# K of one more unit by transposing DMA, with the projection of group 1 spread over more slots, in a cached attention kernel on one Trainium2 core

## The chip, the cores and the metric

The kernel runs on one core of one Trainium2 chip. The metric is the device time of one execution in microseconds (us). A profiled execution also has a span, from the first to the last instruction, which is 1.7 to 3.0 us shorter than the time; so spans are compared where a difference of 1 us matters. Runs are called slow where their time is over 1.5% above the fastest of the same kernel, else fast; verdicts use fast runs only. On one core nothing shows whether a slow run is a state of the chip or a wait of the kernel that some runs have and others don't.

## The reference

A query projection, attention over the last 2048 entries of a cache, and an output projection, all in bf16:

```python
B, Sq, D = 8, 32, 1024;  Hq, Hkv, Sk, Dh = 32, 4, 8192, 128
W = min(4096, max(256, Sk // 4))                      # 2048
q = (x @ wq).reshape(B, Sq, Hq, Dh).transpose(0, 2, 1, 3)
k = jnp.repeat(k_cache[:, :, Sk - W:, :], Hq // Hkv, axis=1)
v = jnp.repeat(v_cache[:, :, Sk - W:, :], Hq // Hkv, axis=1)
p = softmax(einsum("bhqd,bhkd->bhqk", q, k) * Dh ** -0.5)
o = einsum("bhqk,bhkd->bhqd", p, v)
return o.transpose(0, 2, 1, 3).reshape(B, Sq, Hq * Dh) @ wo
```

A pair of a batch and a KV head is a unit: 32 units, numbered KV head by KV head. Eight units share a KV head, called a group here; each group has its slice of wq.

## The kernel before

A unit has 16 tiles of 128 keys, worked on in four slots of four tiles. K must stand with Dh on the partitions before TensorE can use it, and there are three ways to get it there: TensorE transposes it (units in `PE_T`), the DMA transposes it while loading (most units), or VectorE transposes 32 by 32 blocks and GpSimd moves them to their places (units in `V_T`, the "turned" units). Everything that is not scores and values is put into slots by hand:

```python
N_WARM = (8, 0, 0)
PE_T = (0, 1, 2, 3, 4)
# unit: (loaded with unit, slots of the 4 block transposes, first and last slot of the 16 moves, moves by GpSimd)
V_T = {5: (2, (5, 6, 8, 10), 10, 17, 12),
       **{u: (u - 4, range(4 * u - 16, 4 * u - 12), 4 * u - 13, 4 * u - 4, 16) for u in (8, 11, 14, 17, 20, 23, 26, 29)}}
Q_SLOTS = {1: (17, 31), 2: (38, 54), 3: (69, 83)}     # slots over which a group's projection is spread
...
    def load_unit(self, ui):                           # K and V of one unit, then raw K of turned units, then weights
        ...
        for u, at in V_T.items():
            if at[0] == ui:
                self.load_k(u)
        for p, at in zip(self.weights, W_AT):
            if at == ui:
                p()
...
        for ui, (b, g) in enumerate(self.units):
            if ui:
                self.va_copy(ui)                       # VectorE: V into the layout with a column of ones
            for c in range(NCH):                       # one slot
                ...                                    # 4 score matmuls, the exponential on ACT
                while len(pv_queue) > 2:
                    pv_queue.pop(0)()                  # 8 value matmuls of two slots earlier; at a unit's end VectorE normalises
                ...                                    # transposes of the next unit's K, if it is in PE_T
                for p in plan[ui * NCH + c]:           # projections first, then blocks and moves
                    p()
```

VectorE and GpSimd work through their own instructions in the order of the program. Where VectorE waits for one thing, everything behind it waits too (2.76 us in e7_mended below); this is what the whole case turns on. Raw K is K as it was loaded, before it is turned; PSUM is the memory that TensorE writes its results to.

Of the kernel before, what the change touches and what calls it, by code (L numbers as in the profile page):

```python
# [11 lines left out]
BF16 = mybir.dt.bfloat16  # L12
FP32 = mybir.dt.float32
# [6 lines left out]
N_WARM = (8, 0, 0)  # L20
# [3 lines left out]
PE_T = (0, 1, 2, 3, 4)  # L24

V_T = {5: (2, (5, 6, 8, 10), 10, 17, 12),
       **{u: (u - 4, range(4 * u - 16, 4 * u - 12), 4 * u - 13, 4 * u - 4, 16) for u in (8, 11, 14, 17, 20, 23, 26, 29)}}
W_AT = (3, 3, 4, 4, 8, 8, 9, 9, 11, 12, 13, 13, 14, 15, 16, 16, 18, 19, 19, 20, 22, 22, 23, 24, 25, 26, 28, 28)

Q_SLOTS = {1: (17, 31), 2: (38, 54), 3: (69, 83)}  # L30
# [74 lines left out]
class Fast:  # L105
# [101 lines left out]
    def load_unit(self, ui):  # L207

        if ui < len(self.units):
            if ui not in V_T:  # L210
                self.load_k(ui, None if ui in PE_T else 0)
            self.load_v(ui, self.nc.sync)
            if ui not in V_T and ui not in PE_T:
                self.load_k(ui, 1)
        for u, at in V_T.items():
            if at[0] == ui:
                self.load_k(u)
        for p, at in zip(self.weights, W_AT):
            if at == ui:
                p()  # L220
# [46 lines left out]
    def q_pieces(self, g):  # L267
        nc, P, DC = self.nc, self.P, self.DC
        st = {}

        def piece(hl, i):
            if i == 0:
                st["ps"] = self.ps_m.tile([P, 512], FP32, name="q_ps", tag="m")
            for c in range(i * DC // 2, (i + 1) * DC // 2):
                nc.tensor.matmul(st["ps"][:, 0:self.NQ], lhsT=self.wq_t[g, i][:, c % (DC // 2), hl * P:(hl + 1) * P],  # L275
                                 rhs=self.xT[:, c, :], start=(c == 0), stop=(c == DC - 1))
            if i == 1:
                nc.vector.tensor_copy(out=self.q_view(g)[:, :, hl, :],  # L278
                                      in_=st["ps"][:, 0:self.NQ].rearrange("p (b s) -> p b s", b=self.B))
        return [lambda h=h, i=i: piece(h, i) for h in range(self.rep) for i in range(2)]  # L280
# [31 lines left out]
    def start(self):  # L312
        nc, P = self.nc, self.P
# [3 lines left out]
        xf = self.x.rearrange("b s d -> (b s) d")  # L317
# [3 lines left out]
        nc.scalar.dma_start(out=x_sb[:, 1, :], in_=xf[P:2 * P, :])  # L321
# [25 lines left out]
        warm_up(N_WARM[0])  # L347


        def x_turn(half, pl, tag):  # L350
            ps = pl.tile([P, H, self.NT, P], BF16, name="xT_ps", tag=tag)
            for c in range(H):
                for t in range(self.NT):
                    nc.tensor.transpose(ps[:, c, t, :], x_sb[:, t, half * H + c:self.D:self.DC], self.ident[:, :])  # L354
            for i, copy in ((0, nc.vector.tensor_copy), (1, nc.scalar.copy)):
                c0 = half * H + i * H // 2
                copy(out=self.xT[:, c0:c0 + H // 2, :], in_=ps[:, i * H // 2:(i + 1) * H // 2, :, :].rearrange("p c t s -> p c (t s)"))

        x_turn(0, self.ps_m, "m")
        x_turn(1, self.ps_s, "s_ps")  # L360
# [18 lines left out]
        for c in range(self.DC):  # L379
            for h in range(self.rep):  # L380
                q_mm(c, h, 0, P if c >= Q_CUT else self.NQ)
            if c == 0:
                warm_up(N_WARM[2])
                warm_sb = self.c1.tile([P, 8], BF16, name="warm_sb")
                nc.vector.tensor_copy(out=warm_sb[:, :], in_=warm[:, 0:8])
            if c == self.DC - 3:
                tp = self.ps_s.tile([P, KT, P], BF16, name="kf_ps", tag="s_ps")
                k_turn(0)
                k_copy(0)
# [266 lines left out]
```

## Time and profile before

| | before |
|---|---|
| time, median of three runs | 185.55 us (185.06 to 186.25) |
| span of the profiled run | 183.3 us |
| TensorE busy | 178.7 us, 98% |
| ACT, VectorE, GpSimd busy | 131.6, 114.8, 94.7 us |
| first projection matmul, slot 0, unit 8, end of TensorE | 5.84, 12.92, 52.01, 180.53 us |

A row of the timeline reads: start, duration, engine, source line, operation, what it writes and what it reads, how many; then in brackets the idle time before it and what ended it. The starts of matmuls are measured and their ends are modelled, so I measure a wait of TensorE from start to start, less what the matmul itself takes; it comes out about 0.16 us longer than the bracket. The rows that matter are shown in the prediction.

### The profile page before, as it was taken

Reading aid. Unit: us, or ns where it says so; the run is one execution under the profiler, and the core shown is the slowest. Engines: PE = TensorE matmul, PEld = TensorE weight load, DVE = VectorE, ACT = ScalarE, POOL = GpSimd, SP = SyncE. Lnnn points to the kernel's source line nnn. Section 1 sums busy time; section 2 is a strip of 40 time slices with the busy share of each in tenths; the row PEclk is TensorE's granted clock in tenths of the full one; section 3 lists DMA queues with packets and bytes.
Section 4 is the critical chain, followed back from the end, with each engine's and each line's share of the span. In section 5 each row is a group of like instructions: output and inputs, shape, how many; then the busy total and the mean of one; then the engine's idle time right before and its main releaser. Section 6 shows DMA issues by size and latency. Waiting matters only on the chain.

```text
span 183.3 us, 5041 instructions
## 1 busy us (share of the span) xinstructions
PE 178.7 (98%) x2041; PEld 153.6 (84%) x2057; DVE 114.8 (63%) x266; ACT 131.6 (72%) x133; POOL 94.7 (52%) x150
## 2 busy tenths in 40 slices
PE   7999999999999999999999999999999999999993
PEld 2899999999999999987878999987787888888843
DVE  0238899975584774685567558647755865365363
ACT  2218999777799877777786687787877888888800
POOL 2000019759839959929945980896299279600000
DMA  6999999999999999999999999989999999960003
GB/s 173 392 405 407 397 402 367 186 249 397 258 307 303 384 240 325 401 246 249 378 380 227 374 389 224 245 327 386 242 371 345 216 272 286 229 185 1 0 32 93
DMA packets 52954, 51.73 MB, mean 282 GB/s; under 512 B 39744, under 2 KB 40256, under 8 KB 52928
## 3 DMA queue, kind: packets, MB, share of 16 engines
q1 hardware_dynamic: 52352, 50.90, 98.3%
q10 hardware_dynamic: 576, 0.49, 0.8%
q8 instruction: 16, 0.26, 0.6%
q14 instruction: 10, 0.08, 0.1%
HBM read 41.42 MB, written 0.52 MB: 229 GB/s over the span
## 4 chain that ended last, share of the span: by engine, by line
PE 96%; DMA 2%; issue 1%; DVE 0%
PE o_ps L478 32%; PE s_ps L467 31%; PE op_ps L295 14%; PE q_ps L275 11%; PE q_ps L375 4%; DMA x_sb<-in_x_dram 2%; PE tp L236 2%; PE xT_ps L354 1%; PE kf_ps L368 1%; DVE o_t L305 0%; PE cnt_ps L532 0%
## 5 line engine op out<-in xcount | busy, mean ns | idle before, releaser
L469 ACT ACTIVATE pT<-s_ps 128x1024 bf16<-128x1024 f32 x128 | 128.8, 1025 | 32.4 <-PE s_ps L467 31.4
L261 POOL TENSOR_SCALAR kTv<-kb 32x512 bf16<-32x512 bf16 x140 | 93.7, 670 | 63.8 <-PE s_ps L467 37.3
L478 PE MATMUL o_ps<-va,pT 128*128 128x129 bf16 x1024 | 78.8, 220 | 0.1
L478 PEld LDWEIGHTS <-pT 128*128 128x128 bf16 x1024 | 68.5, 98 | 3.1
L467 PE MATMUL s_ps<-QT,kT 128*128 128x256 bf16 x368 | 55.2, 273 | 0.2
L467 PEld LDWEIGHTS <-kT 128*128 128x128 bf16 x368 | 34.8, 98 | 10.3
L295 PE MATMUL op_ps<-wo_sb,OT 128*128 128x512 bf16 (+2 forms) x128 | 32.7, 352 | 0.6
L275 PE MATMUL q_ps<-xT,wq_sb 128*128 128x256 bf16 x192 | 28.1, 273 | 0.0
L409 DVE COPY va<-v_sb 128x2048 bf16<-128x2048 bf16 x32 | 25.3, 789 | 0.1
L251 DVE STREAM_TRANSPOSE kb<-k_raw 128x512 bf16<-128x512 bf16 x36 | 23.8, 685 | 0.0
L415 DVE RECIPROCAL RL_all<-o_ps 128x2 f32<-128x2 f32 x32 | 5.2, 164 | 27.5 <-PE o_ps L478 27.5
L467 PE MATMUL s_ps<-QT,kTv 128*128 128x256 bf16 x144 | 21.6, 272 | 0.0
L420 DVE TENSOR_SCALAR o_sb<-o_ps,RL_all 128x128 bf16<-128x128 f32 x64 | 19.5, 346 | 1.1
L467 PEld LDWEIGHTS <-kTv 128*128 128x128 bf16 x144 | 13.9, 98 | 5.1
L278 DVE CAST QT<-q_ps 128x256 bf16<-128x256 f32 x24 | 9.8, 406 | 13.4 <-PE q_ps L275 13.4
L275 PEld LDWEIGHTS <-wq_sb 128*128 128x128 bf16 x192 | 17.0, 98 | 1.2
L422 DVE STREAM_TRANSPOSE OT<-o_sb 128x256 bf16<-128x256 bf16 x32 | 14.3, 445 | 1.1
L295 PEld LDWEIGHTS <-OT 128*128 128x128 bf16 x144 | 11.4, 98 | 2.3 <-DVE OT L422 0.2
L302 DVE TENSOR_TENSOR oacc<-op_ps,oacc 128x512 f32<-128x512 f32 x8 | 5.5, 682 | 7.4 <-PE op_ps L295 7.4
L375 PE MATMUL q_ps<-xT,wq_sb 128*128 128x256 bf16 (+1 forms) x80 | 7.7, 251 | 0.0
L375 PEld LDWEIGHTS <-wq_sb 128*128 128x128 bf16 x80 | 6.7, 98 | 0.7
L236 PE MATMUL tp<-ident,k_raw 128*128 128x128 bf16 x64 | 5.9, 219 | 0.0
(30 smaller groups left out, 36.6 us busy)
## 6 DMA issues: line engine op xcount, KB each, us to landing
v_sb<-in_v_cache_dram SPq DMA_DIRECT2D x30, 512.0 KB, 7.0
wo_sb<-in_wo_dram SPq DMA_DIRECT2D x16, 512.0 KB, 6.5
wq_sb<-in_wq_dram SPq DMA_DIRECT2D x13, 512.0 KB, 7.3
k_raw<-in_k_cache_dram SPq DMA_DIRECT2D x13, 512.0 KB, 5.9
wq_sb<-in_wq_dram SPq DMA_DIRECT2D x6, 256.0 KB, 4.6
v_sb<-in_v_cache_dram SPq DMA_DIRECT2D x4, 256.0 KB, 4.8
kT<-in_k_cache_dram SPq DMA_TRANSPOSE x36, 6.5
k_raw<-in_k_cache_dram SPq DMA_DIRECT2D x2, 256.0 KB, 5.8
```

The costliest lines, as they stand in the source:

```text
L251: nc.vector.transpose(out=st["kb"][:, sl, :], in_=self.k_raw[ui][:, sl, :])
L261: nc.gpsimd.tensor_scalar(out=out, in0=in_, scalar1=1.0, scalar2=1.0, op0=ALU.mult, op1=ALU.mult)
L275: nc.tensor.matmul(st["ps"][:, 0:self.NQ], lhsT=self.wq_t[g, i][:, c % (DC // 2), hl * P:(hl + 1) * P], rhs=self.xT[:, c, :], start=(c == ...
L278: nc.vector.tensor_copy(out=self.q_view(g)[:, :, hl, :], in_=st["ps"][:, 0:self.NQ].rearrange("p (b s) -> p b s", b=self.B))
L295: nc.tensor.matmul(ps[:, 0:w], lhsT=self.OT[:, gq, c, t * P:(t + 1) * P], rhs=self.wo_t[gq][:, c, n0:n0 + w], start=(k == 0), stop=(k == 7))
L375: nc.tensor.matmul(qs[h // 2][:, h % 2, n0:n1], lhsT=self.wq_t[0, c // H][:, c % H, h * P:(h + 1) * P], rhs=self.xT[:, c, n0:n1], start=(c ...
L409: self.nc.vector.tensor_copy(out=self.va[ui % 3][:, :, 0:self.Dh], in_=self.v_sb[ui][:, :, :])
L420: nc.vector.tensor_scalar(out=o_sb[:, qt, :, :], in0=o_ps[:, qt, 0:Dh].rearrange("p (i c) -> p c i", c=4), scalar1=rl[:, ui * QT_N + qt:ui ...
L422: nc.vector.transpose(out=self.OT[:, g * QT_N:(g + 1) * QT_N, :, b * self.Sq:(b + 1) * self.Sq], in_=o_sb[:, :, :, :])
L467: nc.tensor.matmul(s_ps[:, jj, :], lhsT=self.kT[ui][:, c * CJ + jj, :], rhs=q_u, start=True, stop=True)
L469: nc.scalar.activation(out=pT[:, :, :], in_=s_ps[:, :, :], func=ACT.Exp, bias=0.0, scale=self.scale)
L478: nc.tensor.matmul(o_ps[:, qt, 0:self.VW], lhsT=pT[:, jj, qt * P:(qt + 1) * P], rhs=va[:, j, 0:self.VW], start=(j == 0 and qt == 0), stop= ...
```

## The change

The intent: take 16 transposes from TensorE, the bound. K of unit 4 goes through the transposing DMA. That takes longer (K and V of unit 4 landed in 3.0 us instead of 2.6 in e5_k4_alone), and so, it seems, group 1's weights are loaded ahead of the raw K of the turned units, and the projection of group 1 starts three slots earlier and needs the second half of the weights later (first half for four heads, then second half). The turned units' blocks and moves move one slot back, unit 8's three. Separately, x is loaded and turned by row tiles, and a warm-up matmul goes.

```diff
-N_WARM = (8, 0, 0)
+N_WARM = 7
-PE_T = (0, 1, 2, 3, 4)
+PE_T = (0, 1, 2, 3)
 V_T = {5: (2, (5, 6, 8, 10), 10, 17, 12),
-       **{u: (u - 4, range(4 * u - 16, 4 * u - 12), 4 * u - 13, 4 * u - 4, 16) for u in (8, 11, 14, 17, 20, 23, 26, 29)}}
+       8: (4, range(19, 23), 22, 30, 16),
+       **{u: (u - 4, range(4 * u - 15, 4 * u - 11), 4 * u - 12, 4 * u - 4, 16) for u in (11, 14, 17, 20, 23, 26, 29)}}
-Q_SLOTS = {1: (17, 31), 2: (38, 54), 3: (69, 83)}
+Q_SLOTS = {1: (14, 31), 2: (38, 54), 3: (69, 83)}
 # load_unit: the loop over self.weights now stands before the loop over V_T
 # q_pieces: two heads share a PSUM bank and one cast
-                     st["ps"] = self.ps_m.tile([P, 512], FP32, name="q_ps", tag="m")
+                     st[k] = self.ps_m.tile([P, 2, self.NQ], FP32, name="q_ps", tag="m")
 ...
+        n = 4 if g == 1 else 2
+        return [... for h0 in range(0, self.rep, n) for i in range(2) for h in range(h0, h0 + n)]
 # start
-        nc.scalar.dma_start(out=x_sb[:, 1, :], in_=xf[P:2 * P, :])
+        nc.sync.dma_start(out=x_sb[:, 1, :], in_=xf[P:2 * P, :])
 ...
+        def x_turn(t):
+            ps = self.ps_s.tile([P, 2, self.DC, P], BF16, name="xT_ps", tag="s_ps")
             for i, copy in ((0, nc.vector.tensor_copy), (1, nc.scalar.copy)):
+                for c in range(H):
+                    nc.tensor.transpose(ps[:, i, c, :], x_sb[:, t, i * H + c:self.D:self.DC], self.ident[:, :])
+                copy(out=self.xT[:, i * H:(i + 1) * H, t * P:(t + 1) * P], in_=ps[:, i, 0:H, :])
```

## The prediction

> **What bounds the kernel now.** I read the page first: the busy line and the chain that ended last.
>
> ```profile
> PE 178.7 (98%) x2041; PEld 153.6 (84%) x2057; DVE 114.8 (63%) x266; ACT 131.6 (72%) x133; POOL 94.7 (52%) x150
> ...
> PE 96%; DMA 2%; issue 1%; DVE 0%
> ```
>
> TensorE is busy for 98% and is 96% of the chain, so nothing but TensorE's own work, and the 4.5 us before it can begin, makes the time. Next I read TensorE in order of time, since a share of busy time does not say whether it runs at its rate.
>
> ```profile
> 28.55 0.60 PE L467 MATMUL s_ps<-QT,kT 128*128 128x256 bf16 x4
> 28.99 0.62 PE L478 MATMUL o_ps<-va,pT 128*128 128x129 bf16 x8
> 29.44 0.39 PE L236 MATMUL tp<-ident,k_raw 128*128 128x128 bf16 x4
> 29.66 0.60 PE L467 MATMUL s_ps<-QT,kT 128*128 128x256 bf16 x4
> ```
>
> I call four score matmuls, the eight value matmuls of two chunks earlier and whatever is woven in between a slot; a unit has four slots (unit u starts at slot 4u). Start to start, scores take 0.44 us, values 0.45, four transposes 0.22: a bare slot is 0.89 us, one with four transposes 1.11, one with four projection matmuls (0.44) 1.33. I followed all 128 slots and found no wait over 0.03 us; where 0.22 us seemed lost, a first output-projection matmul is missing from the records. The change can thus win only work taken from TensorE and an earlier start, and it loses wherever a feeder's slack is used up. The slack is in the other engines' timelines. GpSimd, which assembles the turned K of units 5, 8, 11, ..., 29 (the last line from near the end of the run):
>
> ```profile
> 27.03 8.77 POOL L261 TENSOR_SCALAR kTv<-kb 32x512 bf16<-32x512 bf16 x12 [25.46 <-PE s_ps L467]
> 38.44 11.77 POOL L261 TENSOR_SCALAR kTv<-kb 32x512 bf16<-32x512 bf16 x16 [2.64 <-PE s_ps L467]
> 53.18 11.65 POOL L261 TENSOR_SCALAR kTv<-kb 32x512 bf16<-32x512 bf16 x16 [2.97 <-DVE kb L251]
> ```
>
> ```profile
> 147.41 11.74 POOL L261 TENSOR_SCALAR kTv<-kb 32x512 bf16<-32x512 bf16 x16 [4.21 <-DVE kb L251]
> ```
>
> Each assembly is 16 moves, 11.7 us, and starts when VectorE has finished the fourth block transpose of that unit. Unit 8's ends at 50.21 and TensorE reads it at 52.01 (slack 1.8 us); unit 29's ends at 159.15 and is read at 159.85 (slack 0.7):
>
> ```profile
> 52.01 0.60 PE L467 MATMUL s_ps<-QT,kTv 128*128 128x256 bf16 x4
> ```
>
> ```profile
> 159.85 0.60 PE L467 MATMUL s_ps<-QT,kTv 128*128 128x256 bf16 x4
> ```
>
> VectorE, nearly full from 20 to 40 us:
>
> ```profile
> 27.82 1.04 DVE L409 COPY va<-v_sb 128x2048 bf16<-128x2048 bf16 x1
> ...
> 35.77 0.39 DVE L278 CAST QT<-q_ps 128x256 bf16<-128x256 f32 x1
> 36.08 1.28 DVE L251 STREAM_TRANSPOSE kb<-k_raw 128x512 bf16<-128x512 bf16 x2
> 37.29 0.39 DVE L278 CAST QT<-q_ps 128x256 bf16<-128x256 f32 x1
> 37.59 0.69 DVE L251 STREAM_TRANSPOSE kb<-k_raw 128x512 bf16<-128x512 bf16 x1
> ```
>
> The V copy of unit 3 ends at 28.86 and is read by the value matmul at 28.99: slack 0.1 us. Unit 8's fourth block ends at 38.28, and GpSimd starts 0.15 later. Last, the head:
>
> ```profile
> 0.75 3.70 DMA x_sb<-in_x_dram
> 4.50 1.33 PE xT_ps L354 x16
> 5.84 5.40 PE q_ps L375 x48
> ```
>
> **What the Trainium skill says.** "TensorE: Matmul & The Clock Gate", section "Back-to-back issue gap", gives N/2.4 + 2.5 ns warm: 109 ns for 256 columns, 56 for 128. The trace agrees (0.44 us for four scores). Its Part 1 gives N/1.2 while the array is cold; the eight warm-up matmuls of 512 start 427 ns apart, and x's transposes go from 118 to 62 ns apart near 4.8 us, so the changed kernel's earlier first transposes may still be cold. "SBUF — State Buffer", section "Who interferes with whom", says that a VectorE copy in a two-port mode and a GpSimd instruction shut each other out for a whole instruction. The trace agrees: V copies take 0.65 us alone and 1.04 beside GpSimd, and a move grows from 0.61 to about 1.0. "DMA: Bandwidth & Descriptors", "Latency and other measured facts", has 261 GB/s for a DMA transpose with a non-contiguous dimension; here halves of 256 KB land 0.8 to 2.4 us after the transfer before them, where 512 KB of plain K takes 1.3.
>
> **The change part by part.** I read the waits of the changed program from its instruction order and semaphores.
>
> *x by row tiles.* Both tiles now share one queue, so tile 0 should land near 3.9 us (both land at 4.45 and 4.63 now; 256 KB take about 0.65) and tile 1 near 4.6. But each tile's PSUM buffer is now filled in two halves with VectorE's copy of the first half between, and the second four transposes wait for that copy. Per copy: 0.26 us from the start of the last transpose to the copy (5.11 to 5.37 now), 0.425 for the copy, 0.05 back. The chain: 3.95, + 0.24 to 0.36 to the fourth transpose, + 0.74, + 0.42 to the eighth transpose of the next batch, + 0.74, + 0.24 for four more: the projection starts at 6.35 to 6.5 instead of 5.84. **+0.55 us.** The removed warm-up matmul (0.43) is before x arrives and is worth nothing by itself.
>
> *K of unit 4.* 16 transposes of 56 ns leave TensorE: **-0.89 us**, 0.45 of it in slots 12 and 13, 0.45 in slots 14 and 15 (in whose place projection comes earlier, the same work). Two VectorE copies of 0.65 go too. The DMA side: two transposed halves cost 1.6 to 3 us instead of 1.3; K of unit 4 should land by 29 to 31 us and is read from 31 on, its second half two slots later, so it should not be waited for. ACT follows two short slots: its exponentials went 0.91 us apart at slots 33 to 37, which cost TensorE only 0.03 a slot.
>
> *Who pays for shorter slots 12 and 13.* VectorE's work up to the V copy of unit 3 is the same, in the same order, tied to the end of unit 0. TensorE now wants it 0.45 us earlier; slack was 0.1. **+0.37 us** of waiting in slot 14.
>
> *Group 1 over slots 14 to 29.* Same 64 matmuls. Casts are one per two heads: four of about 0.6 us by their spacing (448 columns: 0.53 now) for eight of 0.31.
>
> *Unit 8's K.* This is the large term. Its blocks move from slots 16 to 19 to slots 19 to 22, and in VectorE's order blocks three and four now stand behind unit 4's normalisation and the second cast, which wait for slot 21's value and projection matmuls. I count from the start of slot 22 (S). Value matmuls of slot 21 done at S - 0.25; VectorE, just done with block two, does the normalisation (1.22 us in the trace from reciprocal to the end of the transpose), ending at about S + 1.2; cast 0.6; blocks 0.61 + 0.69; 0.15 to GpSimd: start at S + 3.25. Sixteen moves: 11.75, and 0.05 to TensorE: S + 15.05. Without a wait TensorE reaches unit 8 after eight slots of 1.327 and two of 0.89: S + 12.4. **Wait +2.65 us** (in the kernel before GpSimd starts at S - 0.3). All sixteen moves are needed, since every score contracts over all of them.
>
> *Later turned units.* Their blocks and moves are one slot later. Units 14 to 26 have 2.4 us or more of slack against about 1.2. Unit 11 is helped by unit 8 being late. Unit 29 has 0.7: its fourth block goes behind the V copy of unit 26, from 146.52 to about 147.7, so GpSimd runs to about 160.3: **+0.5 us.**
>
> *Weights ahead of raw K; casts in pairs in groups 2 and 3.* Nothing on the path.
>
> Sum: 0.55 - 0.89 + 0.37 + 2.65 + 0.5 = **+3.2 us**, 185.55 to about 188.7. I put it at 188.6.
>
> **The rivals.** (1) *The intended gain*: TensorE stays full, the transposes go (-0.9) and x arriving by rows gives -0.3: 184.4 us. For it speaks that TensorE is the bound and that the author set unit 8's slots by hand; against it, slot 22 to unit 8 leaves 12.4 us for a GpSimd job of 11.7 that cannot start before S + 2.2 even with VectorE idle. So I hold this for very unlikely. (2) *A DMA wait in place of the one removed*: the two transposed halves sit early in a saturated stream (about 400 GB/s to 32 us), and if they took 2.4 us each, the second half of group 1's weights would land near 34.5 us, where slot 18 wants it: up to 1 us more; unit 8's last blocks stand behind that projection on VectorE, so the later wait would not swallow it: 189.6. (3) *Waits that overlap less badly*: if VectorE is through with unit 4's normalisation sooner and GpSimd meets fewer V copies, the wait for unit 8 is 1.5 us and unit 29 comes out even: 187. (4) *The clock*: a gap of over 3 us on TensorE could throttle it again; at 2.65 us I expect not; with it 190.5.
>
> **Range and chances.** The terms I am least sure of are unit 8 (1.3 to 3.2), the head (0.3 to 0.8) and unit 29 (0 to 0.9). Together they span 186.9 to 189.8 for 8 in 10. Two per cent slower begins at 189.3, under one sigma above my figure: 0.24. Faster by 2% would need 181.8, more than the removed work: 0.01. Within 2%: 0.75.
>
> **What would show it.** In the changed profile: L467 on kTv at unit 8 preceded by an idle TensorE of about 2.6 us released by GpSimd; GpSimd's second run of 16 moves starting about 3 us after slot 22; VectorE's x copies with TensorE idle some 0.7 us before two batches of transposes, and the first q_ps matmul near 6.4; a wait of some 0.4 us on the V copy of unit 3; no wait on a DMA at unit 4. I am wrong if GpSimd's second run starts by about 41 us, or if TensorE shows no idle time before unit 8.

## The result, and the profile after

The changed kernel took 191.41 us (median of four runs, 190.13 to 193.17, one of them slow; a fifth took 190.28) against 185.31 (184.82 to 186.25) for the kernel before on the same chip. The ratio is 1.029, 95% interval 1.021 to 1.037: slower. Ratios here are the mean time of one kernel's fast runs over that of the other's of the same rounds, so they are not quite the ratio of the medians. I had predicted 188.6 and a range up to 189.8.

The page of the changed kernel, busy time, the row of TensorE's load in 40 slices, the granted clock, and the chain:

```profile
PE 181.5 (95%) x2024; PEld 155.1 (81%) x2040; DVE 112.7 (59%) x252; ACT 131.9 (69%) x133; POOL 94.0 (49%) x150
...
PE   7899999999949999999999999999999999999993
...
PEclk9999999999996999999999999999999999999999
...
PE 84%; POOL 6%; DVE 5%; issue 2%; ACT 1%; ACTq 0%
```

TensorE has 17 instructions less and is busy 2.8 us longer. There is a hole in slice 12, the clock is down in the slice after it, and GpSimd and VectorE are now in the chain. In the kernel before TensorE was 96% of it and there was no row of the clock at all. The row tells nothing of the head, since the profile records the clock only from its first change on; there the spacing of the matmuls tells. The hole, in the timeline of the changed kernel (VectorE, GpSimd, TensorE):

```profile
42.75 0.65 DVE L280 CAST QT<-q_ps 128x512 bf16<-128x512 f32 x1
43.32 1.28 DVE L252 STREAM_TRANSPOSE kb<-k_raw 128x512 bf16<-128x512 bf16 x2
44.75 11.95 POOL L262 TENSOR_SCALAR kTv<-kb 32x512 bf16<-32x512 bf16 x16 [6.50 <-issue]
56.76 0.61 PE L466 MATMUL s_ps<-QT,kTv 128*128 128x256 bf16 x4 [2.61 <-POOL kTv L262]
57.66 0.94 PE L466 MATMUL s_ps<-QT,kTv 128*128 128x256 bf16 x4
58.39 1.07 PE L477 MATMUL o_ps<-va,pT 128*128 128x129 bf16 x8
```

Slot 22 starts at 41.59. GpSimd's second run starts 3.16 us after it (it started at 38.44, 0.3 before slot 22, in the kernel before), so unit 8 begins 2.77 us late by start to start. Then the same eight value matmuls that took 0.62 us take 1.07. The table of stretches says why; its eighth column is the granted clock:

```profile
core 0: us, PE busy (x) PEld busy (x) DVE busy (x) ACT busy (x) POOL busy (x), PEclk, DMA share, GB/s
...
57.77:61.18 3.41, 3.41 (x26) 2.93 (x24) 1.61 (x5) 2.51 (x3) 3.10 (x6) 0.50 1.30 143
```

For 3.41 us after the wait TensorE ran at half its clock. The head, in the same timeline:

```profile
3.72 0.63 PE L359 MATMUL xT_ps<-ident,x_sb 128*128 128x128 bf16 x4
4.39 0.42 DVE L360 COPY xT<-xT_ps 128x512 bf16<-128x512 bf16 x1 [0.26 <-PE xT_ps L359]
4.87 1.01 PE L359 MATMUL xT_ps<-ident,x_sb 128*128 128x128 bf16 x8 [0.52 <-DVE xT L360]
...
6.40 0.59 PE L359 MATMUL xT_ps<-ident,x_sb 128*128 128x128 bf16 x4 [0.51 <-DVE xT L360]
...
6.78 3.48 PE L378 MATMUL q_ps<-xT,wq_sb 128*128 128x256 bf16 x16
```

The two waits for VectorE's copy are there, and the projection starts at 6.78. But 16 of its matmuls take 3.48 us, 0.21 each, where they took 0.11: the clock is released (from half to full rate) only at 9.98, the first change on record. And the wait for the V of unit 3 in slot 14 (0.37 by start to start):

```profile
31.42 0.61 PE L477 MATMUL o_ps<-va,pT 128*128 128x129 bf16 x8 [0.21 <-DVE va L408]
```

Where the 7.3 us between the two profiled spans (183.3 and 190.6) come from, by landmarks of TensorE:

| stretch | before | after | difference | made of |
|---|---|---|---|---|
| start to slot 0 | 12.92 | 15.43 | +2.51 | 0.94 later start, 1.57 half clock |
| slot 0 to 14 | 15.63 | 15.18 | -0.45 | eight transposes gone |
| slot 14 to 22 | 10.19 | 10.98 | +0.79 | +0.37 wait, -0.45 transposes, +0.87 two projection pieces done earlier |
| slot 22 to unit 8 | 13.27 | 15.17 | +1.90 | +2.77 wait, -0.87 the same two pieces |
| unit 8 to slot 127 | 120.22 | 122.22 | +2.00 | +1.60 half clock (slots 33 to 35), +0.44 wait at unit 29 |
| slot 127 to the end | 11.07 | 11.62 | +0.55 | after TensorE's end |

Three of the other four runs of the changed kernel had spans of 188.4 to 188.7, the fourth 190.2 (this is the one called slow: its time is 2.97 us longer than its span); so the profiled one is at the long end. The head is the part that varies from run to run in the experiments; the other four were not profiled.

### The profile page after: what moved, and what is told of

Same layout as the page of the kernel before. It is cut to its first block, busy times and chain, and to the rows that moved or that the text cites. A ratio compares the mean times of both kernels' runs of the same rounds, so it can differ in the third digit from the quotient of the medians.

```text
span 190.6 us, 4997 instructions
## 1 busy us (share of the span) xinstructions
PE 181.5 (95%) x2024; PEld 155.1 (81%) x2040; DVE 112.7 (59%) x252; ACT 131.9 (69%) x133; POOL 94.0 (49%) x150
## 4 chain that ended last, share of the span: by engine, by line
PE 84%; POOL 6%; DVE 5%; issue 2%; ACT 1%; ACTq 0%
PE o_ps L477 27%; PE s_ps L466 26%; PE op_ps L298 14%; PE q_ps L277 9%; POOL kTv L262 6%; PE q_ps L378 4%; PE warm_ps L349 2%; DVE kT L239 1%; DVE kb L252 1%; PE xT_ps L359 1%; DVE va L408 1%; DVE o_sb L419 1%; PE tp L237 1%; ACT pT L468 1%; PE kf_ps L371 0%
## 5 line engine op out<-in xcount | busy, mean ns | idle before, releaser
L477 PE MATMUL o_ps<-va,pT 128*128 128x129 bf16 x1024 | 79.7, 221 | 0.3 <-DVE va L408 0.2
L477 PEld LDWEIGHTS <-pT 128*128 128x128 bf16 x1024 | 69.3, 99 | 3.7 <-issue 0.4
L466 PE MATMUL s_ps<-QT,kTv 128*128 128x256 bf16 x144 | 22.5, 281 | 2.9 <-POOL kTv L262 2.6
L466 PEld LDWEIGHTS <-kTv 128*128 128x128 bf16 x144 | 14.1, 101 | 8.6 <-POOL kTv L262 3.5
L277 PEld LDWEIGHTS <-wq_sb 128*128 128x128 bf16 x192 | 16.9, 98 | 1.1
L280 DVE CAST QT<-q_ps 128x512 bf16<-128x512 f32 x12 | 8.0, 669 | 7.8 <-PE q_ps L277 7.8
L378 PE MATMUL q_ps<-xT,wq_sb 128*128 128x256 bf16 (+1 forms) x80 | 9.2, 278 | 0.0
L378 PEld LDWEIGHTS <-wq_sb 128*128 128x128 bf16 x80 | 7.5, 108 | 1.4
L375 DVE COPY kT<-kf_ps 128x1024 bf16<-128x1024 bf16 x2 | 1.4, 692 | 8.2 <-PE kf_ps L371 8.2
```

The costliest lines, as they stand in the source:

```text
L277: nc.tensor.matmul(st[k][:, hl % 2, :], lhsT=self.wq_t[g, i][:, c % (DC // 2), hl * P:(hl + 1) * P], rhs=self.xT[:, c, :], start=(c == 0 a ...
L280: nc.vector.tensor_copy(out=self.q_view(g)[:, :, 2 * k:2 * k + 2, :].rearrange("p b h s -> p h b s"), in_=st[k][:, :, :].rearrange("p h (b ...
L378: nc.tensor.matmul(qs[h // 2][:, h % 2, n0:n1], lhsT=self.wq_t[0, c // H][:, c % H, h * P:(h + 1) * P], rhs=self.xT[:, c, n0:n1], start=(c ...
L466: nc.tensor.matmul(s_ps[:, jj, :], lhsT=self.kT[ui][:, c * CJ + jj, :], rhs=q_u, start=True, stop=True)
L477: nc.tensor.matmul(o_ps[:, qt, 0:self.VW], lhsT=pT[:, jj, qt * P:(qt + 1) * P], rhs=va[:, j, 0:self.VW], start=(j == 0 and qt == 0), stop= ...
```

## The experiments

Seventeen kernels ran; all gave correct results. Medians are of all runs, ratios of fast runs. The kernel before ran along in each set: 185.22 in the first (the first four rows), then 185.97 (four), 186.11 (two), 185.29 (two), 185.33 (three), 185.59 (two).

| run | median us | ratio (95% interval) | TensorE's waits in the profiled run, us |
|---|---|---|---|
| e1_copies_after | 189.74 | 1.024 (1.016 to 1.031) | slot 14 0.37, unit 8 2.77, unit 29 0.42 |
| e2_warm8 | 190.71 | 1.029 (1.024 to 1.034) | the same, and two of 0.72 in the head |
| e3_blocks_early | 188.44 | 1.015 (1.012 to 1.019) | slot 14 0.37, slot 22 0.60, unit 11 1.14, unit 29 0.42 |
| e4_fill | 188.76 | 1.022 (1.016 to 1.028) | slot 14 0.37, unit 29 0.20 (unit 8 filled) |
| e5_k4_alone | 187.09 | 1.005 (0.999 to 1.010) | slot 14 0.36, slot 17 2.34 |
| e6_head_alone | 186.19 | 1.003 (0.999 to 1.007) | the head only |
| e8_k4_late_moves | 186.62 | 1.002 (0.998 to 1.007) | slot 17 0.59 |
| e7_mended | 187.38 | 1.005 (1.000 to 1.009) | slot 19 1.54, slot 31 0.30, slot 58 0.45 |
| e10_k4_weights_first | 186.53 | 0.999 (0.993 to 1.005) | slot 18 0.24, slot 19 0.28 |
| e11_mended_again | 188.39 | 1.010 (1.004 to 1.016) | slot 22 0.20, slot 31 0.29, slot 58 1.95 |
| e12_k4_earlier_blocks | 186.22 | 1.002 (0.998 to 1.006) | slot 11 0.57, slot 58 2.07, slot 70 0.33 |
| e13_unit8_late_alone | 186.04 | 1.004 (1.000 to 1.008) | unit 8 0.96 |
| e14_q_and_unit8 | 190.55 | 1.026 (1.023 to 1.030) | slot 14 1.02, unit 8 2.77 |
| e15_q_alone | 186.49 | 1.005 (1.001 to 1.008) | slot 14 1.02, slot 43 0.19 |
| e16_k4_first_at_4 | 185.44 | 1.000 (0.997 to 1.004) | slot 17 0.17, slot 19 0.28, slot 39 0.80 |
| e17_k4_and_end | 185.59 | 0.999 (0.995 to 1.003) | slot 18 0.26, slot 19 0.29 |
| e18_end_alone | 186.38 | 1.004 (0.999 to 1.008) | slot 12 0.14 |

Slow runs left out of the ratios: one each of e1, e2, e5, e7 and e10, two of six of e8, three of eight of e12; none of the kernel before. The profiled runs of e5 and e12 are among them, with waits over 2 us that belong to the kernel. So these ratios show the kernels at their better, and a ratio near 1 there does not mean that every run is. The table leaves out waits in the head before slot 0, but for e2; they are told below.

### The head and the clock

**e1_copies_after**: the changed kernel, all eight transposes of a row tile before its two copies.

```diff
-            for i, copy in ((0, nc.vector.tensor_copy), (1, nc.scalar.copy)):
+            for i in range(2):
                 for c in range(H):
                     nc.tensor.transpose(ps[:, i, c, :], ...)
+            for i, copy in ((0, nc.vector.tensor_copy), (1, nc.scalar.copy)):
                 copy(...)
```

> The changed kernel with one edit: in x's turn all eight transposes of a tile are issued before the two copies, so TensorE no longer waits for VectorE in the middle of a tile. Theory (the two pauses of 0.7 us, 4.15 to 4.87 and 5.7 to 6.4 us, delay the first projection matmul and leave the clock window too idle to be released before 9.98 us): no pause over 0.4 us, first projection matmul near 5.6 us instead of 6.78, matmuls of 256 columns 109 ns apart from about 6.6 us at the latest, slot 0 at about 12.7 to 13.0 instead of 15.43, time down by 2 to 2.5 us; the wait for unit 8's K stays at 2.5 to 2.9 us. Rival (one warm-up matmul fewer is what keeps the clock low): the pauses go, but matmuls stay 213 ns apart until near 10 us, gain under 1 us.

The two pauses went, the clock was released at 5.24 us, the projection started at 6.02 and slot 0 at 13.55. That is 1.9 us better than the profiled run of the changed kernel and over 0.5 short of what I expected, for two reasons. Tile 1's copy by VectorE (5.54 to 5.96) still stands between the last transpose and the projection, 0.4 us; and a wait of 0.45 us for weights came at 9.51 us, which I had not thought of. The rest of the change, unit 8 included, was as before.

**e2_warm8**: the changed kernel with the eighth warm-up matmul back (`N_WARM = 8`).

> The changed kernel with eight warm-up matmuls as in the kernel before, everything else unchanged. Theory (pauses, not the number of warm-up matmuls): first transposes at 4.2 instead of 3.72 us, pauses unchanged, full clock again only near 10 us; same time or up to 0.5 us longer. Rival (the eighth warm-up matmul releases the clock): 109 ns spacing from the start of the projection, slot 0 near 13.5, 1.5 to 2 us faster. The free-running clock window can make single runs differ by over 1 us, so the profile decides before the times do.

No gain in time: 1.029. But the clock was released at 6.24 here and not near 10, with the same two pauses. My expectation missed that the release moves from run to run by itself. It was at 9.98 in the changed kernel, and at 3.74, 5.18 and 3.81 in e3, e4 and e6, which have the same head; in ten looks at kernels with the old head it lay between 3.75 and 6.66. Slot 0 started at 15.43, 13.57, 13.47 and 13.88 with the new head (mean 14.1), at 13.51 to 13.72 in the three looks with the order of e1, and at 12.77 to 13.46 in eleven with the old head (mean 13.1).

**e6_head_alone**: the kernel before with only the new head (the diff of the change in `start`, and `N_WARM = 7`).

> The kernel before with only the head of the changed kernel (x on one queue, by row tiles, a copy between the two batches of transposes, seven warm-ups). My theory (the two pauses cost 0.6 to 0.9 us, and where the free-running window of the clock falls badly over them, up to 1.6 us of half clock more): first projection matmul at 6.1 to 6.8 instead of 5.84, slot 0 between 13.5 and 15.4 instead of 12.92, times spread over more than 1 us and the median 0.7 to 2 us above before (186 to 187). Rival (the head's loss is made up later, because other engines' feeds get slack): the same time as before, 185.2. A second rival (all runs of it are bad by the full 2.5 us): 187.7 with little spread.

Spans of 183.8 to 185.8 with a median of 184.15, against 183.4 for the kernel before on that chip: +0.75, at the low edge of what I expected; the ratio of 1.003 is hardly outside the noise. So the head costs 0.5 to 1 us, and the 2.51 of the profiled run were a bad fall of the clock. The second rival (always the full 2.5) is out. What it costs with a quick clock is not the pauses alone. In e6 the projection starts only 0.27 us later than before, and then it waits for weights:

```profile
10.29 1.92 PE L375 MATMUL q_ps<-xT,wq_sb 128*128 128x256 bf16 x16 [0.52 <-DMA wq_sb<-in_wq_dram]
```

That is 0.68 us by start to start, and slot 0 is 0.96 late. The piece landed at 10.24; in the kernel before it landed at 8.65 and was wanted at about 9.3. SyncE issues it at 3.55 instead of 3.08, as both tiles of x now stand in front of it; the rest of its delay I can't place. The same wait (0.38 to 0.63 us) is in e1, e3, e7 and e11, and in no look with the old head; where the projection starts at 6.4 or later (e2, e4, the changed kernel) it is not seen. So a quicker start, as in e1, gains little by itself.

**e4_fill**: the changed kernel with dummy matmuls in front of unit 8's first scores, which depend on nothing.

```diff
+                if ui == 8 and c == 0:
+                    fill = self.ps_m.tile([P, 512], FP32, name="fill_ps", tag="m")
+                    for _ in range(12):
+                        nc.tensor.matmul(fill[:, :], ...)     # operands are constant ones
+                    fill_sb = self.c1.tile([P, 8], BF16, name="fill_sb")
+                    nc.vector.tensor_copy(out=fill_sb[:, :], in_=fill[:, 0:8])
```

> The changed kernel with twelve dummy matmuls of 512 columns (2.6 us at full clock) put just before unit 8's first scores, where TensorE waits 2.77 us for GpSimd. Theory (the idle wait itself, not the work after it, halves the clock from 57.77 to 61.18 us): unit 8 starts at the same time (56.6 to 56.9 if the head is as slow as in the profile), but the half-clock window after it is gone: about 1.6 us faster, all of it in slots 33 to 35. Rival (slots 33 to 35 are slow for another reason, such as GpSimd and VectorE sharing a port): those slots stay at 1.6, 1.7 and 1.0 us.

TensorE in e4, around unit 8:

```profile
52.24 2.57 PE L467 MATMUL fill_ps<-const-bfloat16-1.0 128*128 128x512 bf16 x11
54.80 0.61 PE L472 MATMUL s_ps<-QT,kTv 128*128 128x256 bf16 x4
55.24 0.62 PE L483 MATMUL o_ps<-va,pT 128*128 128x129 bf16 x8
```

Unit 8 starts no earlier (41.33 us after slot 0 in both), but behind it TensorE runs at full rate, in all four runs (mean clock 0.998 or more). The median is 2.65 us below the changed kernel's; the profile puts 1.6 of it on the clock and the rest on the head, which fell well here. Useless work in the gap is better than none, so the half clock follows from the idle time and not from anything that unit 8 does. (Twelve matmuls were put in; the profile holds eleven, as some records can be missing.)

How much idle time it takes can be read from the traces. In every trace in which the clock is on record, the stretches between two changes of it are multiples of 3.413 us (51.20 in e14 is 15 of them, 129.71 in the changed kernel is 38). I conclude that the clock is decided window by window; the grid of windows can then be laid from the first release. What lies of a wait in one window:

| kernel | wait | window | idle in it | half clock after it |
|---|---|---|---|---|
| changed | 53.99 to 56.76 | 54.36 to 57.77 | 2.40 | yes |
| e5 | 32.93 to 35.27 | 33.02 to 36.43 | 2.25 | yes |
| e14 | 53.54 to 56.30 | 54.27 to 57.68 | 2.04 | yes |
| e11 | 84.63 to 86.59 | 83.16 to 86.57 | 1.94 | no |
| e1 | 52.11 to 54.87 | 53.02 to 56.44 | 1.85 | no |
| e12 | 84.71 to 86.78 | 85.11 to 88.52 | 1.67 | no |
| e2 | 52.71 to 55.48 | 54.03 to 57.44 | 1.45 | no |

About 2.0 us of idle time in one window halves the next; a wait of 2.77 us does so when the windows fall right. If the windows fall freely, that is the share of positions in which one window holds over 2.0 us of the wait: ((3.413 - 2.77) + 2 x (2.77 - 2.0)) / 3.413 = 64%, an estimate from the numbers of this table. Counted by a mean clock of 0.991 or less it was 13 of 17 runs: five of five of the changed kernel, two of four of e1 and of e2, four of four of e14. Nine of nine against four of eight leaves open whether the windows do fall freely. This table was made after the runs; no run was made to test the limit itself.

The same grid tells when the clock is released in the head. In all 18 traces with a record of it, the release comes at the end of the first window that holds little idle time: 0.86 us at most (e2, one pause and the beginning of the other). Windows before it held 0.95 us or more, the time before the first matmul included. In the changed kernel the window from 3.16 to 6.57 holds both pauses, 1.44 us, and the release is one window late; in e4, with the same pauses, the window from 1.77 to 5.18 holds one of them, 0.72, and the clock is released. This too was read afterwards and not tested by an edit.

### Unit 8, and what the slots really cost

**e3_blocks_early**: the changed kernel with unit 8's blocks and moves where they were.

```diff
-       8: (4, range(19, 23), 22, 30, 16),
+       8: (4, range(16, 20), 19, 28, 16),
```

> The changed kernel with unit 8's block transposes and moves back in slots 16 to 19 and 19 to 28. Theory (blocks three and four stood behind slot 21's cast on VectorE): fourth block done near 40.4 instead of 44.6 us, GpSimd's sixteen moves from 40.6 to 52.3, no wait before unit 8 (TensorE reaches it near 54.0), and no half clock at 57.8 to 61.2; 2.8 + 1.6 = 4.4 us faster in the profile. Rival (unit 8's raw K comes too late, being loaded behind the weights): VectorE stands waiting for that load before block one, and a wait before unit 8 of over 1 us stays.

The wait before unit 8 went, and so did the half clock. But two waits took its place:

```profile
PE s_ps L466 <- POOL kTv L262: 1.0, 1, 1.0
PE o_ps L477 <- DVE va L408: 0.6, 2, 0.4
```

(The columns of this view are the us waited in sum, how often, and the longest; e3 here.) Unit 11 now waits 1.14 us for GpSimd, whose blocks the change had moved back one slot and which the wait of unit 8 had covered; and slot 22 waits for the V of unit 5, since VectorE stood idle 2.05 us until 35.87 for unit 8's raw K. That raw K arrives late because the weights now come first. So of the 4.4 us that unit 8 and the clock had cost in the profile, some 2.5 (1.029 less 1.015, of 185 us) came back.

**e13_unit8_late_alone**: the kernel before with that one line of the change, unit 8 at slots 19 to 22.

> The kernel before with unit 8's blocks at slots 19 to 22 and its moves from slot 22, and nothing else. My theory: the fourth block stands behind unit 4's normalisation and a cast of 0.4 us, GpSimd's second run starts 2.9 to 3.2 us after the start of slot 22, and unit 8 waits 2.4 to 2.8 us. The clock is halved for 3.413 us after it (1.6 us more) in those runs in which a window of 3.413 us of the clock holds over 2.0 us of the wait, which for a free phase is 40 to 60% of the runs: 187.6 to 190 against before's 185.2 to 186. Rival (the wait comes from the wide casts and the late raw K of the whole change, not from the slots): a wait of under 1.5 us.

The rival was right on the size. GpSimd and TensorE in e13:

```profile
41.34 11.44 POOL L262 TENSOR_SCALAR kTv<-kb 32x512 bf16<-32x512 bf16 x16 [5.66 <-PE s_ps L468]
...
52.84 0.61 PE L468 MATMUL s_ps<-QT,kTv 128*128 128x256 bf16 x4 [0.79 <-POOL kTv L262]
```

A wait of 0.96 us, no half clock, +0.4%. So the slots of the blocks alone are a third of the term.

**e14_q_and_unit8** and **e15_q_alone**: the kernel before with the projection of group 1 as the change has it (banks of two heads, slots 14 to 30), with and without unit 8 at slots 19 to 22.

> The kernel before with two parts of the change: group 1 projected over slots 14 to 30 in banks of two heads, and unit 8's blocks at slots 19 to 22. My theory: the wait of 0.96 us that the blocks' slots alone gave grows by the two projection pieces that TensorE has behind it already at slot 22 (0.87), by the wider cast before the fourth block (0.3 to 0.45), and by 0 to 0.45 for one more V copy beside GpSimd's moves: 2.1 to 2.8 us, and in about half of the runs half a clock for 3.413 us after it. Time 187.3 to 189.5 against before's 185.3 to 186. Rival (what made the wait longer in the whole change is the late raw K of unit 8 and the late V of unit 5): the wait is 0.9 to 1.3 us, ratio 1.005.

> The kernel before with group 1 projected over slots 14 to 30 in banks of two heads, unit 8's blocks left at slots 16 to 19. My theory: the projection alone costs nothing, as it is the same 64 matmuls and unit 8's K is started early: no wait over 0.3 us before unit 8 (GpSimd starts at 38.4 to 39, is done by 50.7, and TensorE is there at 51.1 at the earliest or 52.0, depending on where the pieces lie), ratio 0.998 to 1.003. Rival (wide casts and banks of two heads make TensorE wait for PSUM or for the second half of the weights, which lands at 32.2): a new wait of 0.4 us or more between slots 14 and 22, ratio over 1.003.

TensorE in e14:

```profile
56.30 0.61 PE L470 MATMUL s_ps<-QT,kTv 128*128 128x256 bf16 x4 [2.60 <-POOL kTv L262]
...
57.64 1.02 PE L481 MATMUL o_ps<-va,pT 128*128 128x129 bf16 x8
```

The wait is 2.77 us and the half clock behind it is there in all four runs, exactly as in the changed kernel. These two parts together reach 1.026; each alone makes only 1.004 and 1.005. That this is near the whole change's 1.029 is partly luck, since e14 has a wait of 1.02 us in slot 14 (below) where the changed kernel has one of 0.37 for another reason; the proof is the same wait before unit 8, to 0.01 us, and the same half clock. The reckoning from 0.96 to 2.77: TensorE takes 12.39 us from slot 22 to the end of slot 31 instead of 13.27, because two pieces of projection are behind it already (0.88); GpSimd starts 3.16 us after slot 22 instead of 2.72, behind a normalisation of unit 4 that begins 0.21 us later and a cast that takes 0.65 instead of 0.39 (0.44); and its 16 moves end 0.5 us later relative to their start, since they fall on three V copies instead of two. That is the sum of my theory; the split is read from the two traces, and no run has the wide casts without the early pieces. In e15 the rival was right as well, with a wait that my theory had not, 1.02 us in slot 14:

```profile
PE q_ps L276 <- DVE kT L238: 0.9, 1, 0.9
```

The projection in slot 14 wants a PSUM buffer of the pool that unit 4's transposes are still using, and waits for VectorE's copy of K. In the changed kernel unit 4 has no such transposes and there is no such wait. So it seems that the early projection needs K of unit 4 to be out of the way.

### K of unit 4 by DMA

**e5_k4_alone**: the kernel before with `PE_T = (0, 1, 2, 3)`.

> The kernel before with only the K of unit 4 loaded through the transposing DMA. My theory: this part alone is worth the 0.89 us of transposes less about 0.37 us that slot 14 then waits for VectorE's copy of the V of unit 3, so about 184.7 against 185.2 (ratio 0.997), with that one wait in the trace, no DMA wait at unit 4, and no half clock anywhere (no wait near 2 us). Rival (the transposed halves disturb the saturated load stream): a DMA wait appears between slots 16 and 32 and the time is 185.2 or more.

The wait in slot 14 was 0.36 as expected, but the rival came with it. TensorE in e5, at slots 17 and 18:

```profile
35.27 0.39 PE L275 MATMUL q_ps<-xT,wq_sb 128*128 128x256 bf16 x2 [2.18 <-DMA wq_sb<-in_wq_dram]
...
36.38 1.01 PE L275 MATMUL q_ps<-xT,wq_sb 128*128 128x256 bf16 x4
```

The last piece of group 1's weights landed at 35.22, wanted at 32.93, and the half clock followed. In the kernel before the same piece landed at 32.17 and was wanted at about 33.2. The stream of loads is full until about 38 us: K and V of unit 4 together took 3.0 us there instead of 2.6, and two pieces of weights each took about 1.1 us longer than usual in this run (2.29 and 2.57 us after the landing ahead of them instead of 1.3 to 1.4), which I cannot account for; single loads of 512 KB that take 2.6 to 2.7 us stand in other traces too (one landing at 17.82 in the kernel before, one at 35.49 in e8). The next kernel shows another look.

**e8_k4_late_moves**: e5 with VectorE's four moves of unit 5 put behind the copy of the V of unit 3 (`5: (2, (5, 6, 8, 10), 13, 18, 12)`).

> As the kernel with K of unit 4 alone, and with the moves of unit 5 spread over slots 13 to 18, so that VectorE's four of them come behind its copy of the V of unit 3. My theory: the slot-14 wait goes from about 0.37 to under 0.1, and the whole 0.89 us is kept: 184.3 to 184.5 (ratio 0.995). Rival (the moves of unit 5 then end too late, and slot 20 waits): 184.7 or more, with a wait on kTv at unit 5. This would be the version that beats both.

Slot 14 no longer waited. The weights landed at 32.78 and were waited for by 0.59 us in the profiled run; in two of six runs the mean clock was 0.989 and 0.991 (189.8 and 190.0 us, both called slow and not in the ratio), so the wait was probably longer there. No gain: 1.002.

**e10_k4_weights_first**: K of unit 4 by DMA, the loop over the weights ahead of the raw K as in the change, unit 5's moves at slots 12 to 15, unit 8's blocks at `(18, 18, 19, 19)`.

> The kernel before with K of unit 4 by transposing DMA, group 1's weights loaded ahead of the raw K of unit 8 (as the change has it), the moves of unit 5 at slots 12 to 15 and the blocks of unit 8 at slots 18 and 19, ahead of anything that waits for unit 4's last values. The two looks at K of unit 4 without this order waited 2.34 and 0.59 us at slot 17 for the last piece of the weights (landed 35.22 and 32.78, wanted at about 31.9). My theory: with the order turned round it lands one K transfer (1.3 to 2.5 us) earlier, so the wait is 0 to 1 us, no half clock in most runs, unit 8 does not wait (its raw K lands near 34 to 35, GpSimd starts near 38.5, 50.3 at the end against 51.2 wanted), slot 22 may wait up to 0.5 us for the V of unit 5: 184.8 to 186 against before's 185.2 to 186, ratio 0.995 to 1.003. Rival (the K of unit 4 costs the saturated load stream more than its transposes cost TensorE, whatever the order): waits on DMA of 0.9 us or more, ratio 1.003 or more.

The weights came in time (32.00). What was left were 0.24 us for the V copy of unit 4 and 0.28 for unit 5's last move by GpSimd: VectorE had no idle time from 23 to 38 us. Ratio 0.999.

**e12_k4_earlier_blocks**: e10 with unit 5's blocks at `(5, 6, 7, 8)` and moves at 12 to 16.

> As the kernel with K of unit 4 by DMA and the weights first, but the blocks of unit 5 one and two slots earlier (slots 5, 6, 7, 8) and VectorE's four moves of it at slots 12, 14, 15 and 16, so that only three stand before the copy of the V of unit 4 and GpSimd starts sooner. In the run before this one TensorE waited 0.24 us at slot 18 for that copy and 0.28 at the end of slot 19 for GpSimd's last move of unit 5 (27.49 to 36.17). My theory: both waits go to under 0.1, and the profile shows 0.6 to 0.9 us less from slot 0 to the end of TensorE's work than before's 167.6 (180.53 - 12.92): 166.7 to 167.0; time 0.3 to 0.5% under before (the noise from run to run is 1 us, so the verdict will be same). Rival (VectorE, without idle from 23 to 38 us, is the bound there, and the blocks moved forward only push other copies back): a new wait of 0.3 us or more at slots 9 to 14 and 167.3 or more.

The rival was right: those two waits went and one of 0.57 us at slot 11 came, for a copy of K. There was also a wait of 2.07 us at slot 58, in the profiled run, that has nothing to do with unit 5. VectorE in e12:

```profile
82.16 0.71 DVE L252 STREAM_TRANSPOSE kb<-k_raw 128x512 bf16<-128x512 bf16 x1 [4.60 <-DMA k_raw<-in_k_cache_dram]
...
84.28 1.88 DVE L252 STREAM_TRANSPOSE kb<-k_raw 128x512 bf16<-128x512 bf16 x3
86.08 0.65 DVE L410 COPY va<-v_sb 128x2048 bf16<-128x2048 bf16 x1
```

The first block of unit 17 waits 4.6 us for its raw K, which stands behind weights in the queue (it landed at 82.06; in e10, with the same order, at 79.41, and no wait), and the V copy that TensorE needs stands behind it. Three of the eight runs were slow at full clock and are not in the ratio of 1.002.

**e16_k4_first_at_4**: e10 with the order turned round only in unit 4's loads.

> As the kernel with K of unit 4 by DMA and the weights first, with the order turned round for unit 4's loads only. In the last run with the order turned round everywhere, TensorE waited 2.07 us at slot 58, where VectorE's copy of V of unit 14 stood behind a block of unit 17 whose raw K came late behind weights. My theory: no wait at slot 58 in any run, 0.2 to 0.6 us at slots 18 and 19 as before, so TensorE's work from slot 0 to its end is 167.2 to 167.5 (before 167.6), no run over 1% above its fastest but for the launch, ratio 0.996 to 1.002. Rival (K of unit 4 by DMA is a loss by its own disturbance of the loads): waits over 0.9 us in sum and ratio over 1.003.

No wait at slot 58; 0.45 at slots 17 to 19, and a new one of 0.80 for K of unit 10 in slot 39, which the other runs seem not to have (five spans of six at 183.2 to 183.8). Ratio 1.000.

### Mending the changed kernel

**e7_mended**: the changed kernel with the order of e1, unit 8 at slots 16 to 19, the other turned units back by one slot, unit 5's moves at slots 13 to 17.

> The changed kernel with four mends: all transposes of an x tile before its copies, unit 8's blocks and moves back at slots 16 and 19, the other turned units' back by one slot, the moves of unit 5 at slots 13 to 18. My theory: the waits before units 8, 11 and 29 and at slot 14 go (each under 0.1), the wait at slot 22 of about 0.6 us (VectorE: V copy of unit 5 behind a block and a wide cast) stays, the head stays 0.6 behind, K of unit 4 gives 0.9: 185.2 to 186.2 (ratio 1.00 to 1.005), no half clock. Rival (a wait is left that I don't know of, as the wide casts make VectorE late elsewhere): over 187.

187.38: the waits before units 11 and 29 and at slot 14 went and that before unit 8 was down to 0.30, but there was one of 1.54 us at slot 19. VectorE in e7:

```profile
36.06 0.71 DVE L252 STREAM_TRANSPOSE kb<-k_raw 128x512 bf16<-128x512 bf16 x1 [2.76 <-DMA k_raw<-in_k_cache_dram]
...
37.96 0.29 DVE L260 COPY kTv<-kb 32x512 bf16<-32x512 bf16 x1
```

Unit 8's first block waits 2.76 us for raw K, and the last moves of unit 5, which TensorE needs at slot 20, stand behind it.

**e11_mended_again**: e7 with unit 5's moves at slots 12 to 15 and unit 8's blocks at `(18, 18, 19, 19)`.

> The changed kernel with all transposes of an x tile before its copies, the moves of unit 5 at slots 12 to 15, the blocks of unit 8 at slots 18 and 19, and the other turned units' blocks and moves back by one slot. In the mended kernel before this one unit 5 was read 1.54 us late, since VectorE's last moves for it stood behind a block of unit 8 that waited for its raw K (loaded behind the weights, landing near 34.7). My theory: that wait goes, as the four moves of VectorE are now in front; what stays is the head (0.6), up to 0.6 us at slot 22 for the V of unit 5 and 0.45 at slot 58: 185.3 to 186.5, ratio 1.00 to 1.005, no half clock. Rival (blocks at slots 18 and 19 wait for raw K as well and hold the casts of the projection): a wait of over 1 us between slots 18 and 22, ratio over 1.007.

That wait went; slot 22 waited 0.20, and slot 58 waited 1.95 us in the way shown for e12. My theory had 0.45 us there, as in e7; in size the rival's ratio came out (1.010), but for another reason than the rival's.

So the slots that look too late in the change have a reason: with the weights in front, raw K comes late, and blocks put early would hold VectorE. The change pays either on VectorE (early) or on GpSimd (late).

### The end of the program

The twelve kernels with K of unit 4 by DMA that ran before this test take 1.33 to 1.42 us from the landing of the last output to the end of the span, the five without 0.88 to 0.99. SyncE there waits for eight DMA semaphores one after the other; in the first sort the last output has the first of them, and seven waits of 0.06 us follow. DMAs take these semaphores in turn, and the transposed K is two DMAs instead of one.

**e17_k4_and_end**: e16 with one DMA less (V of unit 30 in one, `V_HALVES = 31`). **e18_end_alone**: the kernel before with one DMA more (`V_HALVES = 29`), which leaves everything else as it is.

> The last kernel with K of unit 4 by DMA (order of loads turned round for unit 4 only), with V of unit 30 loaded in one DMA instead of two, so that the number of DMAs is again that of the kernel before. My theory: from the landing of the last output to the end of the span it takes 0.9 us again instead of 1.33, TensorE's work is unchanged: 0.44 us less than the kernel without it, 183.0 to 183.4 us in span and a ratio of 0.995 to 0.999. Rival (the transposing DMA itself lengthens the end): 1.33 us stays, ratio 1.000.

> The kernel before with V of unit 29 loaded in two DMAs instead of one, nothing else: one DMA more. My theory: from the landing of the last output to the end of the span it takes 1.33 us instead of 0.88, and the time is 0.44 us (0.24%) above before. Rival (the end is lengthened by the transposing DMA, not by the number of DMAs): 0.9 us, ratio 1.000.

From the last landing to the end: 0.89 in e17 (183.68 - 182.79) and 1.34 in e18 (185.45 - 184.11). It is the count of DMAs and not the transposing. In time it is too small to be told from the noise: e17 has a ratio of 0.999. It has the lowest span of all (182.7), but it is not shown to beat the kernel before; its median, 185.59, is the same as that of the kernel before beside it.

## Why the prediction was wrong

I held "within 2%" for likeliest (0.75) and gave "slower" 0.24; it came out slower by 2.9%, with the median 1.6 us above the range.

**What held.** The transposes were worth the 0.89 us; slot 14 waited 0.37 as said; GpSimd's second run started 3.16 us after slot 22 (said 3.25) and unit 8 waited 2.77 (said 2.65); unit 29 waited 0.44 (said 0.5); no DMA wait at unit 4. Reading the slack of the feeders from the trace of before, and the order of VectorE's instructions from the changed program, gave these to 0.1 us.

**The step that failed** is in rival 4: "a gap of over 3 us on TensorE could throttle it again; at 2.65 us I expect not". It did, for 3.413 us, in all five runs (by their mean clock of 0.991), and cost 1.6 us in the profile. I had taken the limit as a length of gap from the Trainium skill, "TensorE: Matmul & The Clock Gate", whose table "Why this matters for your kernels" asks for "No PE-idle gaps >~3µs between matmul bursts". A gap of 2.77 us did it here; what fits the traces is idle time within a window, about 2.0 us (e4 shows that it is the idle time; the limit is read from the table of windows). With it as a certain event my sum would have been 190.2. In the three quicker runs (spans of 188.4 to 188.7 against 183.3) 5.1 to 5.4 us were lost where I had 3.1; the half clock's 1.6 and the tail's 0.44 below make up the difference. The profiled run had 1.96 us more than my term in the head as well.

**The head** was mis-sized: "+0.55" as the later start alone. It was 0.75 in e6 and 2.51 in the profiled run. Of the 2.51, 1.57 is a half clock until 9.98. The window from 3.16 to 6.57 holds both pauses (1.44 us), and I take that as the reason that it did not release the clock: in the other looks with pauses the window before the release held at most 0.86 us of them. This fits all the traces but is argued from them; no run was made to show it. Three readings were wrong besides. Tile 0 of x landed at 3.36 and not near 3.9, so that its transposes waited for the warm-up matmuls, and taking one away was not "worth nothing": with it back in e2 they start at 4.15 instead of 3.72, and the projection 0.30 us later. The later weights, 0.68 us in e6, were in no term. And in the kernel before, the step of 118 ns between transposes need not be the clock, since tile 1 landed only at 4.63 there; in the changed kernel they are 107 ns apart, so the first ones were slow, as feared.

**The tail** was missing: 0.44 us for one DMA more (e17, e18), in no term of mine.

**Right for the sum, wrong on the parts.** I wrote of the weights ahead of raw K: "Nothing on the path." No wait shows there in the changed kernel, but it is what shortens the wait for weights that comes with K of unit 4 by DMA (e5 2.34 and e8 0.59 without it, e10 none and e16 0.17 with it, one look each), and it makes raw K late, so that unit 8's blocks could not simply be moved forward again (e3, e7). And I put the 2.65 us on unit 8's slots: alone they give 0.96 (e13), with the projection 2.77 (e14). My working had the two earlier pieces and the wide cast inside it, but not told apart.

Rival 1, the intended gain, is answered too: K of unit 4 by DMA without the rest comes out even (e10, e16, e17), since VectorE and the load stream were as full as TensorE between 23 and 38 us. Of the 0.89 us that TensorE gained, waits of 0.45 to 0.6 took the larger part, and the tail 0.44 where it was not mended.

## What to carry to other kernels

When the engine at the bound loses work in a stretch, look first whether its feeders have any slack in that stretch; if VectorE and the loads are as full as it is, the gain turns into waits. A step that looks costly alone may be there to pay for another one, so undo parts in pairs as well as singly: two parts of 0.4% and 0.5% made 2.6% here. And reckon any wait of TensorE above 2 us at its length plus the half clock that may follow (1.6 us here), or fill it.

## What the Trainium skill lacked or had wrong

- "TensorE: Matmul & The Clock Gate", Part 1 and section "HAM oscillation — how this bites in real kernels": it states the free-running window of 3413 ns, which the traces confirm (all stretches are multiples of 3.413 us). But its rule that the clock falls after at least one idle window, "no PE-idle gaps >~3.4µs", is too mild: 2.04, 2.25 and 2.40 us of idle time within a window halved it, 1.94 and less did not.
  The page also puts the spread of the release at 500 ns by the phase (a box there does say that the number of slow matmuls is "run-variable"); it came between 3.75 and 6.66 us with the old head here, and once at 9.98 where TensorE paused twice for 0.72 us. How much idle time a window may hold and still release the clock is not stated; here windows with up to 0.86 us did, and windows with 0.95 us or more did not.
- What one DMA more can do at the end of a program is on no page that I found. Eight semaphores taken in turn and waited for one after the other made it 0.44 us (1.34 against 0.89 us from the last landing to the end).
